# An elementwise kernel of large transfers: the second load is issued after a VectorE memset

## The chip, the cores and the metric

The kernel runs on one core of a Trainium2 chip. The metric is device time in microseconds (us) of one execution; three runs of the kernel before gave a median of 150.7 us (150.7 to 150.88). The time stands beside a profile of one further execution, taken by the hardware profiler.

## The reference

```python
B, S, D = 512, 32, 640          # bf16 x and fx, alpha one bf16 number
def reference(x, fx, alpha):
    return x + alpha * fx
```

Each input has 10,485,760 elements in bf16, so 20.97 MB of x and as much of fx are read, and 20.97 MB of output are written.

## The kernel before

The arrays are taken as flat. A **unit** is 512 bf16 numbers (1 KiB) on each of 128 partitions, 128 KiB in all; an input is 160 units. All data goes through one SBUF tile `room` of 207 units (line 83). The whole order of work is written out by hand in the string `PLAN` (lines 30 to 54), and a loop (line 114) turns each step into one instruction; no scheduler moves them. The instructions of one engine run in the order of the plan, and between engines the framework adds the waits that the data needs.

- `f 8 63 @ 152` loads units 8 to 62 of fx to places 152 and up of the room, `x ...` loads x, and `s ...` stores from the room. All of them are DMAs issued by SyncE (line 109), so they go into one queue, in this order. A word `after + 184` at the end makes the issue wait for the step `+ 184` (helper `late`, line 91).
- `a` loads alpha (line 98), sets a row `ones` with a VectorE memset of 128 numbers (line 101) and spreads alpha over the partitions with one small matmul (line 103) and a copy to `a_f` (line 104).
- `m 144 63` multiplies 63 units at place 144 by alpha, in place, on VectorE (line 122).
- `+ 0 144 38` adds 38 units at place 144 to those at place 0, on VectorE (line 144).
- `p` and `q` (lines 127 and 139) move 14 units of scaled fx aside to PSUM and add them from there.

The work is done in three stretches of the arrays, cut at units 0, 63, 124 and 160 (`CUTS`): fx is loaded and scaled, x is loaded and fx added to it, and the sum is stored from the place of x. The room is too small for all, so places are used again: the loads from the fourth large one on wait for adds that free their place. Each DMA has 128 rows, one a partition. The first steps of the plan are what matters here: a load of 8 units of fx (1 MiB) to places 144 to 151, then a load of 55 units of fx (7040 KB), alpha, 63 units of x, and 61 units of fx, none of which waits for anything.

Places 124 to 129 of the room are first written by the step `f 124 160 @ 110`, and nothing reads them before that.

Of the kernel before, what the change touches and what calls it, by code (L numbers as in the profile page):

```python
# [1 line left out]

# [4 lines left out]

ALU = mybir.AluOpType
F32 = mybir.dt.float32
I32 = mybir.dt.int32  # L10

K = 512
P = 128
ROOM = 207
CUTS = (0, 63, 124, 160)
KEPT = 14

PLAN = """  # L30
f 0 8 @ 144
f 8 63 @ 152
a
x 0 63 @ 0
m 144 63
f 63 124 @ 63
+ 0 144 38
x 63 99 @ 146
+ 38 182 25
x 99 124 @ 182  # L40
m 63 61
p 110 14
f 124 160 @ 110
+ 146 63 36
x 124 160 @ 63
+ 182 99 2
m 110 36
+ 184 101 9
s 0 63 @ 0 after + 184
q 193 14  # L50
s 63 124 @ 146
+ 63 110 36
s 124 160 @ 63
"""


@with_exitstack
def kernel(
    ctx: ExitStack,
    tc: tile.TileContext,  # L60
    x: bass.AP,
    fx: bass.AP,
    alpha: bass.AP,
    out: bass.AP,
):
    nc = tc.nc
    flat = {
        name: t.rearrange("b s d -> (b s d)") for name, t in (("x", x), ("f", fx), ("s", out))
    }
    assert flat["x"].shape[0] == P * CUTS[-1] * K  # L70

    def stretch(what, a, b):
        low, high = next(c for c in zip(CUTS, CUTS[1:]) if c[0] <= a < c[1])
        rows = flat[what][P * low * K : P * high * K].rearrange("(p n) -> p n", p=P)
        return units(rows, a - low, b - low)

    consts = ctx.enter_context(tc.tile_pool(name="consts", bufs=1))
    psum = ctx.enter_context(tc.tile_pool(name="psum", bufs=1, space=bass.MemoryType.PSUM))
    rooms = ctx.enter_context(tc.tile_pool(name="rooms", bufs=1))
    ctx.enter_context(tc.manual_schedule())  # L80

    kept = psum.tile([P, KEPT * K], x.dtype, name="kept")
    room = rooms.tile([P, ROOM * K], x.dtype, name="room")
    a_f = consts.tile([P, 1], F32, name="a_f")
    info = mybir.DependencyInfo(mybir.DependencyClass.Sync, mybir.DependencyReason.DATA)
    done, moved = [], {}

    def units(t, a, b):
        return t[:, a * K : b * K]

    def late(r, after):
        if after:
            what, a = after[1], int(after[2])
            tc.add_manual_dep(r.ins, moved[what, a].ins.name, info, reason="issued late")

    def spread_alpha(after):
        a_1 = consts.tile([1, 1], alpha.dtype, name="a_1")
        done.append(nc.sync.dma_start(out=a_1[:], in_=alpha[None, :]))  # L98
        late(done[-1], after)
        ones = consts.tile([1, P], alpha.dtype, name="ones")  # L100
        nc.vector.memset(ones[:], 1.0)  # L101
        a_ps = psum.tile([P, 1], F32, name="a_ps")
        done.append(nc.tensor.matmul(a_ps[:], ones[:], a_1[:], start=True, stop=True))  # L103
        nc.vector.tensor_copy(out=a_f[:], in_=a_ps[:])  # L104

    def transfer(what, a, b, at, after):
        away, here = stretch(what, a, b), units(room, at, at + b - a)
        out, in_ = (away, here) if what == "s" else (here, away)
        r = nc.sync.dma_start(out=out, in_=in_)  # L109
        late(r, after)  # L110
        moved[what, a] = r
        done.append(r)

    for step in PLAN.strip().split("\n"):
        what, *rest = step.split()
        if what == "a":
            spread_alpha(rest)
        elif what == "m":
            t, n = map(int, rest)
            f = units(room, t, t + n)  # L120
            done.append(
                nc.vector.tensor_scalar(out=f, in0=f, scalar1=a_f[:], scalar2=None, op0=ALU.mult)  # L122
            )
        elif what == "p":
            t, n = map(int, rest)
            done.append(
                nc.vector.tensor_scalar(  # L127
                    out=units(kept, 0, n).bitcast(I32),
                    in0=units(room, t, t + n).bitcast(I32),
                    scalar1=0,  # L130
                    scalar2=None,
                    op0=ALU.bitwise_or,
                )
            )
        elif what == "q":
            t, n = map(int, rest)
            xt = units(room, t, t + n)
            done.append(
                nc.vector.tensor_tensor(out=xt, in0=xt, in1=units(kept, 0, n), op=ALU.add)  # L139
            )  # L140
        elif what == "+":
            t, u, n = map(int, rest)
            xt, f = units(room, t, t + n), units(room, u, u + n)
            moved[what, t] = nc.vector.tensor_tensor(out=xt, in0=xt, in1=f, op=ALU.add)  # L144
            done.append(moved[what, t])
        else:
            a, b, _, at = rest[:4]
            transfer(what, int(a), int(b), int(at), rest[4:])

    last = nc.sync.nop(nofuse=True)  # L150
    for i in done[:-1]:
        tc.add_manual_dep(last.ins, i.ins.name, info, reason="all but the last store")


# [1 line left out]
_INS = ['x', 'fx', 'alpha']  # L156
_OUTS = [((512, 32, 640), 'bfloat16')]


# [23 lines left out]
```

## Time and profile before

| | us |
|---|---|
| median of three runs | 150.70 |
| the profiled execution | 150.75 |
| its span (first to last instruction of the engines) | 149.0 |
| DMA packets, as a share of 16 engines' span | 98.0% |
| bytes moved | 62.92 MB in 1586 packets |
| VectorE busy | 69.4 (47%) |

The profile page divides the span in 40 slices and gives, for each, how busy an engine is in tenths; the DMA row is the mean over the 16 DMA engines of the core. The windows view gives the same for any stretch: after the stretch and its length come the busy time of each engine with its number of instructions, then the granted TensorE clock, the DMA share and the GB/s. A packet is counted in the stretch in which it starts, with its whole size and its whole time; so a short stretch can show a share over 1, and the bytes of a stretch divided by 8192 count the packets of the first load, whose rows have 8192 bytes. In the timeline and in the chain of work, times are us from the start of the span; SPq is SyncE's sequencer, which issues the DMAs.

### The profile page before, as it was taken

To read this page: it belongs to the slowest core of one execution; us is meant where nothing else is said; L and a number is where in the kernel's file an instruction comes from. 1 tells how busy PE (TensorE), PEld (TensorE's weight loads), DVE (VectorE), ACT (ScalarE), POOL (GpSimd) and SP (SyncE) were. 2 spreads that over 40 slices of the span, in tenths; PEclk is the share of its full clock that TensorE was granted. 3 is DMA by queue.
4 is the path that set the end of the run, shared out by engine and by line. 5 is a ranking of instruction groups with operands and counts; after the bars stand their busy time and mean duration, and the time that the engine had idled before them with its cause. 6 is when DMAs were issued, how large, how long until landed. Compare 5 with 4: busy or idle time off the path is not lost.

```text
span 149.0 us, 80 instructions
## 1 busy us (share of the span) xinstructions
PE 0.2 (0%) x1; PEld 0.1 (0%) x1; DVE 69.4 (47%) x13; POOL 0.2 (0%) x4
## 2 busy tenths in 40 slices
PE   0000000000000000000000000000000000000000
PEld 0000000000000000000000000000000000000000
DVE  0000009920099996999999009999950000000000
POOL 0000000000000000000000000000000000000000
DMA  5996998996969969989999989999696998969993
GB/s 176 590 439 287 484 519 364 468 537 294 546 268 537 520 285 427 475 376 422 419 454 475 445 346 475 475 436 554 277 554 277 546 419 386 537 268 427 475 475 158
DMA packets 1586, 62.92 MB, mean 422 GB/s; under 512 B 178, under 2 KB 178, under 8 KB 178
## 3 DMA queue, kind: packets, MB, share of 16 engines
q1 hardware_dynamic: 1586, 62.92, 98.0%
HBM read 41.94 MB, written 20.97 MB: 422 GB/s over the span
## 4 chain that ended last, share of the span: by engine, by line
DMA 38%; DVE 27%; DVEq 7%; another core or an unknown queue 1%; SPq 1%; issue 0%
DMA room<-in_x_dram 26%; DVE room L144 13%; DMA room<-in_fx_dram 11%; DVE room L122 9%; DVEq L178 7%; DVE kept L127 3%; DVE room L139 2%; SPq L109 1%; SPq L98 0%; DVEq L122 0%; DVEq L144 0%
## 5 line engine op out<-in xcount | busy, mean ns | idle before, releaser
L144 DVE TENSOR_TENSOR room<-room 128x18432 bf16<-128x18432 bf16 (+4 forms) x6 | 39.7, 6641 | 10.4 <-DMA room<-in_x_dram 10.4
L122 DVE TENSOR_SCALAR room<-room,a_f 128x32256 bf16<-128x32256 bf16 (+2 forms) x3 | 22.0, 7331 | 8.4 <-DMA room<-in_fx_dram 8.3
L104 DVE COPY a_f<-a_ps 128x1 f32<-128x1 f32 x1 | 0.2, 157 | 21.1 <-PE a_ps L103 21.1
L127 DVE TENSOR_SCALAR kept<-room 128x3584 int32<-128x3584 int32 x1 | 3.9, 3894 | 0.0
L139 DVE TENSOR_TENSOR room<-room,kept 128x7168 bf16<-128x7168 bf16 x1 | 3.9, 3881 | 0.0
L101 DVE MEMSET ones<- 1x128 bf16 x1 | 0.2, 165 | 0.8 <-PEq L167 0.8
L103 PE MATMUL a_ps<-a,ones 1*128 1x1 bf16 x1 | 0.2, 158 | 21.9 <-DMA a<-in_alpha_dram 21.9
L167 POOL MEMSET const-uint8-127<- 128x1 uint8 x1 | 0.1, 102 | 0.0
L167 POOL MEMSET const-bfloat16-1.0<- 128x1 bf16 x1 | 0.1, 101 | 0.0
L103 PEld LDWEIGHTS <-ones 1*128 1x128 bf16 x1 | 0.1, 98 | 1.0 <-DVE ones L101 1.0
L167 POOL MEMSET const-float32-0.0<- 128x1 f32 x1 | 0.1, 98 | 0.2 <-issue 0.2
L167 POOL MEMSET const-float32-1.0<- 128x1 f32 x1 | 0.1, 98 | 0.0
## 6 DMA issues: line engine op xcount, KB each, us to landing
room<-in_x_dram SPq DMA_DIRECT2D x2, 4608.0 KB, 18.7
room<-in_x_dram SPq DMA_DIRECT2D x1, 8064.0 KB, 39.1
out_dram<-room SPq DMA_DIRECT2D x1, 8064.0 KB, 22.3
room<-in_fx_dram SPq DMA_DIRECT2D x1, 7808.0 KB, 57.2
out_dram<-room SPq DMA_DIRECT2D x1, 7808.0 KB
room<-in_fx_dram SPq DMA_DIRECT2D x1, 7040.0 KB, 20.9
room<-in_fx_dram SPq DMA_DIRECT2D x1, 4608.0 KB, 17.1
out_dram<-room SPq DMA_DIRECT2D x1, 4608.0 KB, 38.1
```

The costliest lines, as they stand in the source:

```text
L101: nc.vector.memset(ones[:], 1.0)
L103: done.append(nc.tensor.matmul(a_ps[:], ones[:], a_1[:], start=True, stop=True))
L104: nc.vector.tensor_copy(out=a_f[:], in_=a_ps[:])
L109: r = nc.sync.dma_start(out=out, in_=in_)
L122: nc.vector.tensor_scalar(out=f, in0=f, scalar1=a_f[:], scalar2=None, op0=ALU.mult)
L127: nc.vector.tensor_scalar(out=units(kept, 0, n).bitcast(I32), in0=units(room, t, t + n).bitcast(I32), scalar1=0, scalar2=None, op0=ALU.bit ...
L139: nc.vector.tensor_tensor(out=xt, in0=xt, in1=units(kept, 0, n), op=ALU.add)
L144: moved[what, t] = nc.vector.tensor_tensor(out=xt, in0=xt, in1=f, op=ALU.add)
L167: nc = _bacc.Bacc("TRN2", target_bir_lowering=False, num_devices=1)
L178: with _tile.TileContext(nc) as tc:
```

## The change

A new kind of step, `w t n`, clears n units from place t with a VectorE memset. One such step is put behind the first load, and the second load waits for it. Everything else in the plan stays.

```diff
 PLAN = """
 f 0 8 @ 144
-f 8 63 @ 152
+w 124 6
+f 8 63 @ 152 after w 124
 a
 x 0 63 @ 0
 m 144 63
...
                 nc.vector.tensor_scalar(out=f, in0=f, scalar1=a_f[:], scalar2=None, op0=ALU.mult)
             )
+        elif what == "w":
+            t, n = map(int, rest)
+            moved[what, t] = nc.vector.memset(units(room, t, t + n), 0.0)
         elif what == "p":
```

In the compiled program the memset is VectorE's first instruction, ahead of the memset of `ones`, and is written as 128x1536 (6 KiB a partition, so elements of 4 bytes). On SyncE the order of DMAs is the same as before, and only the second DMA has a new wait.

## The prediction

> **What bounds the kernel now.** I read the page's DMA rows first. The 16 DMA engines are busy nearly all the time, on one queue, so a gain or loss must come from the stretch before their first packet, the one behind their last, or a pause or slowness between.
>
> ```profile
> DMA  5996998996969969989999989999696998969993
> ...
> q1 hardware_dynamic: 1586, 62.92, 98.0%
> ```
>
> The reader is to see the 5 of the first slice and the 98.0%: 98.0% of 149.0 us is 146.0 us of packets on each engine, and 3.0 us without. VectorE, the only other engine with work, is busy 47%. Next the start, since the change is there: the chain of work, in order of time (start, length, what), gives SyncE's first two issues, and the timeline (the same columns) what is issued behind them.
>
> ```profile
> 0.73 0.38 SPq L109
> ...
> 1.17 0.42 SPq L109
> ```
>
> ```profile
> 0.81 0.17 DVE L101 MEMSET ones<- 1x128 bf16 x1 [0.81 <-PEq L167]
> ...
> 1.64 0.33 SPq L98 DMA_DIRECT2D a<-in_alpha_dram  x1
> 2.01 0.35 SPq L109 DMA_DIRECT2D room<-in_x_dram  x1
> 2.40 0.45 SPq L109 DMA_DIRECT2D room<-in_fx_dram  x1
> 21.87 0.16 PE L103 MATMUL a_ps<-a,ones 1*128 1x1 bf16 x1 [21.87 <-DMA a<-in_alpha_dram]
> ```
>
> Then the windows view over the first 5 us, to see when the first load's packets run and when the second's begin.
>
> ```profile
> 0.00:1.74 1.74, 0.00 (x0) 0.10 (x1) 0.17 (x1) 0.20 (x4) 1.00 0.00 0
> 1.74:2.00 0.26, 0.00 (x0) 0.00 (x0) 0.00 (x0) 0.00 (x0) 1.00 2.22 410
> 2.00:2.50 0.50, 0.00 (x0) 0.00 (x0) 0.00 (x0) 0.00 (x0) 1.00 0.65 197
> 2.50:3.00 0.50, 0.00 (x0) 0.00 (x0) 0.00 (x0) 0.00 (x0) 1.00 0.77 295
> 3.00:3.50 0.50, 0.00 (x0) 0.00 (x0) 0.00 (x0) 0.00 (x0) 1.00 1.00 410
> 3.50:4.00 0.50, 0.00 (x0) 0.00 (x0) 0.00 (x0) 0.00 (x0) 1.00 1.01 426
> 4.00:4.57 0.57, 0.00 (x0) 0.00 (x0) 0.00 (x0) 0.00 (x0) 1.00 0.98 417
> 4.57:5.10 0.53, 0.00 (x0) 0.00 (x0) 0.00 (x0) 0.00 (x0) 1.00 4.12 1778
> ```
>
> No packet starts before 1.74 us, which is 1.01 us behind the start of the first issue (0.73). GB/s times length gives the bytes started, and those over 8192 the packets of the first load: 13, 12, 18, 25, 26 and 29 in the six stretches from 1.74 on, 123 of its 128 by 4.57. The last stretch's 942 KB are the other 5 (41 KB) and 16 of 56,320 bytes (901 KB): all 16 engines go over to the second load between 4.57 and 5.10 us. That load was issued at 1.17, so its packets stood ready about 2.18 (1.17 + 1.01) and waited 2.4 us or more for the engines. **This 2.4 us is the cover of the change.**
>
> **The memset.** No row has this operation at this size. From below: the memset of `ones` took 0.165 us, and 6 KiB can't take less. From above: if all of those 165 ns went with its 128 elements, one is 1.29 ns, and 1536 are 1.98 us (3.96 us for 3072, if it went by bf16). The nearest row by element size is the int32 operation of line 127, 3894 ns for 3584, which is 1.087 ns each: 1536 x 1.087 = 1.67 us. I take 1.67. The Trainium skill ("VectorE: DVE Perf Modes", section "Zero memsets can be issued as uint32 (trn2)") says that a memset takes one cycle an element whatever the type; by its clock of 0.96 GHz an estimate is 1.60 us, and the sum would be the same.
>
> **The issue.** VectorE's first instruction starts at 0.81, so the memset ends at about 2.48. SyncE sees it a little later (the chain shows 0.02 us between the end of VectorE's line 127 at 71.93 and the issue at 71.95; I take 0.05): the second load is issued at 2.53 instead of 1.17, 1.36 us late. Its packets stand ready at 2.53 + 1.01 = 3.54. The engines take them from 4.57 on: 1.03 us are left, and the wait costs **nothing**. Without that cover it would cost up to 1.36 us.
>
> **What is queued behind the waiting instruction.** On SyncE: alpha (1.64 to about 3.00), 63 units of x (2.01 to 3.37) and 61 of fx (2.40 to 3.76). None is wanted soon. Alpha's packet comes behind the second load's on its engine and lands at 21.87, by then the issue is long past. x starts behind 8064 KB of fx: at 431 GB/s (below) 19.2 us, so at some 21 us; fx behind it near 40. On VectorE: the memset of `ones` moves from 0.81 to about 2.5, and the weight load on TensorE behind it from 1.03 to about 2.7; both wait for alpha at 21.87 anyway. VectorE's next instruction is the copy at 22.06, after 21.1 us of idleness. The cleared places are next written by a load issued at 71.95; it already waits for later VectorE steps. So the cost is nothing there too, with 17 us or more of cover.
>
> **What a later issue does to the first load's packets.** Here the trace shows something that the change could take away. DMA share times length times 16, over the packets, is the mean time of one: 0.71, 0.43, 0.34, 0.32 us in the first four stretches against 0.31 in the last two. The excess, 13 x 0.40 + 12 x 0.12 + 18 x 0.03 + 25 x 0.01 = 7.4 us, is 0.46 us on each of 16 engines. It falls in 1.74 to 3.1 us, just while SyncE issues the next four DMAs (1.17 to 2.85). Two readings: the engines start cold, or issuing disturbs them. For the second, look at issues in mid-run:
>
> ```profile
> 51.50:53.50 2.00, 0.00 (x0) 0.00 (x0) 2.00 (x2) 0.00 (x0) 1.00 1.16 500
> ...
> 71.90:73.90 2.00, 0.00 (x0) 0.00 (x0) 2.00 (x2) 0.00 (x0) 1.00 0.98 422
> 81.60:83.60 2.00, 0.00 (x0) 0.00 (x0) 0.57 (x1) 0.00 (x0) 1.00 0.77 332
> ```
>
> GB/s over share is the rate while busy: 431, 431 and 431, in stretches that begin with an issue (51.57, 71.95, 81.60), as in one without (98.60 to 101.00: 430 at 1.00). In the four stretches at the start it is 185, 303, 383 and 410. So an issue in mid-run slows nothing, though large packets may hide there what small ones show. And the issues don't go away: they move to 2.53 to 4.2 us, over the rest of the same load. I take the excess as a cold start that stays, **0**, and keep both ends: a gain of 0.46 if the whole excess is due to the issues and vanishes, a loss of as much if it comes a second time.
>
> **The sum.** 150.75 + 0 (wait, covered) + 0 (queued behind it) + 0 (packets at the start) = 150.75 in the profiled execution; against the median of 150.70, 0.05 lower, it is 150.7.
>
> **Rivals.**
> *Quiet start, faster.* With only one load issued, its 16 engines are fed sooner and more evenly. For: the coincidence in time above, and that the end is set by the engine that lags most, so an uneven start is paid in full. Against: the 431 GB/s in mid-run. It must remove 0.30 of the 0.46 us to be seen; about 0.4 gives 150.3. Chance 0.28.
> *The queue runs dry, slower.* At 4.57 to 5.10 us an engine finds no packet of the second load. This decides once memset and issue take over 1.03 us more than I reckoned: a memset over 2.70 us, or a second load that needs over 2.04 us from issue to packet. At 3.96 us for the memset the packets stand ready at 0.81 + 3.96 + 0.05 + 1.01 = 5.83, and the mean engine (dry at 4.83) waits 1.0 us: 151.7. A smaller form: the queue is not dry, but the second load's first packets are as slow as the first load's (13 x 0.40 / 16 = 0.33 us): 151.0. For: nothing here shows a queue filled with 1 us to spare. Against: 1.01 us in the only case seen, and the program's 1536 elements. Chance 0.19, mostly at 151.0 to 151.3.
> *Every delay is paid, slower.* A transfer issued 1.36 us late ends 1.36 us late, as it would where nothing covers it: 152.1. The waiting 2.4 us of the second load speak against it. Chance 0.03. The Trainium skill ("DMA: Bandwidth & Descriptors", section "Rules for kernel authors") speaks for early issue, so that the fixed setup overlaps with other work; by it the change can only lose, and the trace agrees only where a queue has nothing else to move.
> *The wait has no effect*, because the memset is over before SyncE comes to it. It would have to end by 1.17, so take 0.36 us; the time is that of the forecast, 150.7, and its chance is in there.
>
> **How the numbers follow.** A measurement of this kernel can tell about 0.2%, 0.3 us, from no change. The forecast, within 0.2%, has 0.50; faster 0.28; slower 0.19 + 0.03 = 0.22. The range goes from 150.25 (the excess at the start nearly all gone) to 151.2 (the excess twice, 150.7 + 0.46); left out are a pause of half a microsecond or more and the whole delay, about 0.1, and a gain above all that the start holds, under 0.1.
>
> **What would show it.** In the profile after: a VectorE memset from 0.8 to 2.5 us, the second issue at 2.5, and in the windows view all 16 engines going over near 4.6 to 5.1 us, with DMA shares near 1 around it. If the forecast is wrong by the quiet start, packets at 1.74 to 2.5 us show over 300 GB/s while busy; if by the dry queue, the shares from 4.6 to 6 us fall below 1. Later, every landing should keep its time (alpha 21.87, x 41.15) or shift with the start by one amount.

## The result, and the profile after

The changed kernel takes 151.49 us in the median of 22 runs (150.94 to 152.44); the kernel before, on the same chips, 150.74 (150.66 to 151.38). The ratio is 1.005, with a 95% interval of 1.0035 to 1.0064: 0.75 us slower, where I had forecast no change. The spread of the runs has grown too, from 0.7 to 1.5 us. The profiled execution took 151.35 us, its span 149.6, both 0.60 above those of before.

The DMA rows of the page look as before:

```profile
DMA  5998996997969979989999899999696997969993
...
q1 hardware_dynamic: 1586, 62.92, 98.0%
```

98.0% of a longer span is more busy time: 0.980 x 149.6 = 146.6 us a DMA engine against 146.0, for the same bytes. So the loss is not idleness in the main: the same packets took longer (0.46 us an engine of the 0.60, by the trace's packet records, which hold the start, time and size of every packet). The timeline of the first 25 us (start, length, what) shows where the steps moved:

```profile
0.72 2.09 SPq L112 DMA_DIRECT2D room<-in_fx_dram  x2
1.11 1.34 DVE L129 MEMSET room<- 128x1536 uint32 x1 [1.11 <-PEq L173]
2.41 0.17 DVE L104 MEMSET ones<- 1x128 bf16 x1
...
2.86 0.32 SPq L101 DMA_DIRECT2D a<-in_alpha_dram  x1
3.22 0.34 SPq L112 DMA_DIRECT2D room<-in_x_dram  x1
3.61 0.43 SPq L112 DMA_DIRECT2D room<-in_fx_dram  x1
22.20 0.16 PE L106 MATMUL a_ps<-a,ones 1*128 1x1 bf16 x1 [22.20 <-DMA a<-in_alpha_dram]
```

The memset ends at 2.45 us; in the trace the second issue, merged here with the first into one row of x2, starts at 2.48. All this is where I put it (2.48 and 2.53). But alpha, which comes behind the second load's packets, starts the matmul at 22.20 instead of 21.87. So 0.33 us are lost inside the first two loads. The windows view has it:

```profile
1.74:2.00 0.26, 0.00 (x0) 0.00 (x0) 0.26 (x1) 0.00 (x0) 1.00 2.78 473
2.00:2.50 0.50, 0.00 (x0) 0.00 (x0) 0.50 (x2) 0.00 (x0) 1.00 0.15 49
2.50:3.00 0.50, 0.00 (x0) 0.10 (x1) 0.08 (x1) 0.00 (x0) 1.00 1.05 410
...
4.57:5.10 0.53, 0.00 (x0) 0.00 (x0) 0.00 (x0) 0.00 (x0) 1.00 4.32 1747
```

The last row is to be read beside the same stretch of before (4.12, 1778). GB/s over share, the rate while busy, is 404 where it was 432. All 16 engines still go over to the second load between 4.57 and 5.10, without a pause, so by the record nothing is late. But the second load's first packets are **slow**. A packet of 56,320 bytes took 2.08 us in every case of before; here, by the packet records, 9 of the first 16 took longer by over 0.01 us, the slowest by 0.55, and all 16 by 0.15 on average.

The later steps, from the timelines: VectorE's first large add starts at 41.57 (before 41.25, 0.32 later), the multiplication behind the last load of fx at 89.69 (89.15, 0.54 later), and the end is 0.60 later. So just over half of the loss in this execution is there when x has landed. The rest shows after the issue at 72.29 us (before 71.95, 0.34 later). It goes with packets that run at 422 to 428 GB/s while busy in the stretches 52 to 60, 60 to 66 and 66 to 72 us, against 430 to 432 before.

### The profile page after: what moved, and what is told of

It reads as the page before. It is cut to its first block, busy times and chain, and to the rows that moved or that the text cites. A ratio compares the mean times of both kernels' runs of the same rounds, so it can differ in the third digit from the quotient of the medians.

```text
span 149.6 us, 81 instructions
## 1 busy us (share of the span) xinstructions
PE 0.2 (0%) x1; PEld 0.1 (0%) x1; DVE 70.7 (47%) x14; POOL 0.2 (0%) x4
## 4 chain that ended last, share of the span: by engine, by line
DMA 37%; DVE 28%; DVEq 7%; another core or an unknown queue 1%; issue 1%; SPq 0%
DMA room<-in_x_dram 26%; DVE room L150 13%; DMA room<-in_fx_dram 12%; DVE room L125 9%; DVEq L184 7%; DVE kept L133 3%; DVE room L145 2%; DVE room L129 1%; SPq L101 0%; SPq L112 0%; DVE ones L104 0%; DVEq L125 0%; DVEq L150 0%
## 5 line engine op out<-in xcount | busy, mean ns | idle before, releaser
L129 DVE MEMSET room<- 128x1536 uint32 x1 | 1.3, 1338 | 1.1 <-PEq L173 1.1
```

Source lines behind the costliest of these rows:

```text
L129: moved[what, t] = nc.vector.memset(units(room, t, t + n), 0.0)
```

## The experiments

**Lead** is below the time from the start of a load's issue to the start of its first packet. For the second load it was 3.41 us before (1.17 to 4.58) and is 2.19 in the changed kernel (2.48 to 4.67). My forecast stood on 1.01 us being enough. Two theories at first: *in step* (the late issue leaves the 16 engines close together, and so they slow each other) and *late* (the load is issued too near to its turn). The diffs are against the changed kernel.

### Is it the memset, the other issues, the length, or the first load?

The first kernel keeps the memset and drops the wait.

```diff
-f 8 63 @ 152 after w 124
+f 8 63 @ 152
```

> The memset of 6 KiB stays, but nothing waits for it: the second load is issued at 1.17 us as before. Theory 'in step' (with the second issue late, the 16 engines start their packets close together, and engines in step slow each other for the next 65 us): as before, 150.7 us, hardly any packet of the second load above 2.08 us. Theory 'late' (the second load is issued too near to its turn, and its first packets are slow for that): 150.7 us as well. Theory 'memset' (VectorE's writing at the start disturbs the loads): 151.5 us.

Measured: 150.87 us, ratio 0.9998 (0.999 to 1.0007). The memset is free, also where it writes while loads land.

The second one moves the wait to alpha and the two loads behind it.

```diff
-f 8 63 @ 152 after w 124
-a
+f 8 63 @ 152
+a after w 124
```

> The second load is issued at once, and alpha with the two large loads behind it wait for the memset (issues at 2.5 us and later, as in the changed kernel). Theory 'in step': the issue that falls on the first packets (1.74 to 2.5 us) is the second load's own, which is back, so the engines are spread again: 150.7 to 150.9 us. Theory 'late': the second load is early again: 150.7 us. A third theory, that issues at 2.5 to 4 us disturb the packets of that time and of the second load: 151.3 us or more, since three of the four stay late.

Measured: 150.90 us, ratio 1.0001 (0.9992 to 1.0009). The wait costs only where it stands before the second load, though the three behind it are issued at 2.49, 2.84 and 3.23 us.

The third has a memset of 2 KiB.

```diff
-w 124 6
+w 124 2
```

> The memset is 2 KiB a partition (512 elements, some 0.55 us), so the second issue comes at about 1.5 us instead of 1.17 or 2.46. Theory 'late': its packets stand ready 2 us before their turn, so 150.7 us. Theory 'in step': the second load's issue work falls on the first load's second packets instead of the first: between the two, 150.8 to 151.3 us, with a wide spread of runs.

Measured: 150.87 us, ratio 0.9998 (0.999 to 1.0007), with a lead of 3.46 us (the first load took longer in that execution). 'In step' had expected a spread of runs; there is none (150.78 to 151.07).

The fourth keeps the wait and makes the first load twice as large.

```diff
-f 0 8 @ 144
+f 0 16 @ 144
 w 124 6
-f 8 63 @ 152 after w 124
+f 16 63 @ 160 after w 124
```

> The first load is 16 units instead of 8 (its packets then last until about 7.5 us), and the second, of 47 units, still waits for the 6 KiB memset and is issued at 2.46 us. Theory 'late': the cover is 3.5 us instead of 1.1, so the loss goes: 150.7 us. Theory 'in step': the start of the first load is as undisturbed as in the changed kernel, so the engines stay close and the loss stays: 151.2 us or more, a spread of runs of over 0.8 us.

Measured: 150.89 us, ratio 0.9997 (0.9989 to 1.0006). The issue is as late as in the changed kernel, and the packets of the second load start just as close together: 15 of 16 between 7.28 and 7.52 us. But its lead is 4.65 us, and nothing is lost. **'In step' falls here, 'late' stands.**

### Is it really the lead?

With the large first load, a longer memset brings the lead back to what it was.

```diff
-f 0 8 @ 144
-w 124 6
-f 8 63 @ 152 after w 124
+f 0 16 @ 144
+w 124 15
+f 16 63 @ 160 after w 124
```

> The first load is 16 units as in the run that lost nothing, but the memset is 15 KiB a partition (to about 4.85 us), so the second issue comes 2.25 us before the turn of its packets (7.1 us), as in the changed kernel. Theory 'late': the loss comes back, 151.3 to 151.6 us, with slow first packets of the second load. If it stays at 150.9, the lead isn't what decides, but something bound to the first 5 us of the execution or to the 8 small packets per engine.

Measured: 152.05 us, ratio 1.0071 (1.0058 to 1.0084). The lead was 2.37 us, and the loss is back, larger than the 151.3 to 151.6 us expected. The windows view at the change of loads, first for the 16 units with a lead of 4.65 us, then for this kernel:

```profile
7.12:7.52 0.40, 0.00 (x0) 0.00 (x0) 0.00 (x0) 0.00 (x0) 1.00 4.47 1925
```

```profile
7.25:7.76 0.51, 0.00 (x0) 0.00 (x0) 0.00 (x0) 0.00 (x0) 1.00 4.35 1510
```

1925 / 4.47 = 431 GB/s while busy, and 1510 / 4.35 = 347. By the packet records some engines also stood idle here between the two loads, 1.6 us over all 16 together; in the changed kernel none did.

The next one doubles the memset of the changed kernel, so that the engines really run dry.

```diff
-w 124 6
+w 124 12
```

> The memset is twice as long (12 KiB a partition, to about 4.05 us); the second load is issued at 4.06 and by the first load's 1.01 us its packets stand ready at 5.07, where the engines run dry at 4.67 to 5.00. Theory 'late' (the second load must be issued some time, over 2.2 us, before its turn, or its first packets are slow): a larger loss than the changed kernel's 0.75 us, 151.9 to 152.5. Theory 'only a pause counts' (what my forecast stood on): 0.1 to 0.4 us of pause, 151.2 us, below the changed kernel. Theory 'other issues' (the descriptors of alpha and the two large loads, issued 0.4 to 1.6 us behind the second load, disturb its first packets): they fall behind the first packets' start, about 151.5.

Measured: 152.28 us, ratio 1.0091 (1.0078 to 1.0104). The issue started at 4.08, the first packet at 5.05, a lead of 0.97 us. This is the forecast's 1.01 us to the first packet, and it isn't the price. By the packet records the pause between the two loads is 0.40 us on the average engine, as I would have reckoned, but the loss is 1.4. The windows view and the timeline of this kernel:

```profile
5.05:5.90 0.85, 0.00 (x0) 0.00 (x0) 0.00 (x0) 0.00 (x0) 1.00 3.28 1060
```

```profile
42.80 17.02 DVE L150 TENSOR_TENSOR room<-room 128x19456 bf16<-128x19456 bf16 x2 [10.39 <-DMA room<-in_x_dram]
...
90.69 5.02 DVE L125 TENSOR_SCALAR room<-room,a_f 128x18432 bf16<-128x18432 bf16 x1 [6.97 <-DMA room<-in_fx_dram]
```

The row holds the 16 first packets: 0.85 x 3.28 = 2.79 us each on average, 0.71 above 2.08, at 323 GB/s while busy. The slowest, in the packet records, took 1.34 us more. x lands 1.55 us later than before (42.80 against 41.25), the last fx 1.54 (90.69 against 89.15), and the span is 1.6 longer. By the packet records, the last of the 16 first packets ended 0.43 us later than before in the changed kernel and 1.64 later in this one, and x landed 0.32 and 1.55 later. So the end goes by the slowest of 16 engines, not by their mean, and what it loses at the start it hardly makes up.

Two kernels ask whether the issues *behind* the second load do the harm. One moves them away from the start of its first packets, the other brings them up to these (the last issue ends 0.3 us before the first of them) and leaves the second load early.

```diff
 f 8 63 @ 152 after w 124
-a
+w 130 14
+a after w 130
```

> The second load waits for the 6 KiB memset as in the changed kernel (issue at 2.46), and alpha with the loads behind it wait for a second memset of 14 KiB a partition (to about 6.3 us), so that nothing else is issued while the first 16 packets of the second load start. Theory 'late': the loss stays, 151.3 to 151.6 us. Theory 'other issues': it goes, 150.9 us.

```diff
-w 124 6
-f 8 63 @ 152 after w 124
-a
+w 124 9
+f 8 63 @ 152
+a after w 124
```

> The second load is issued at once, and alpha with the two large loads wait for a 9 KiB memset (to about 3.25 us): they are issued at 3.3, 3.6 and 4.0 to 4.5 us, later than in the changed kernel, so that their descriptors come with the first packets of the second load. Theory 'late': 150.9 us. Theory 'other issues': 151.4 us or more.

Measured: 152.16 us (151.01 to 152.63), ratio 1.0078 (1.0051 to 1.0105), for the first, with a lead of 2.27; 150.88, ratio 1.0001 (0.9993 to 1.001), for the second. The first lost more than the 151.3 to 151.6 us expected of 'late', but it lost with the other issues out of the way. 'Other issues' is out.

### How long must the lead be?

```diff
-w 124 6
+w 124 4
```

> The memset is 4 KiB a partition (to about 1.92 us): the second load is issued at 1.93 us, some 2.75 us before its turn at 4.7. So far a lead of 3.3 us or more lost nothing, 2.2 us lost 0.6 to 1.3 us, 1.0 us lost 1.4 us. Theory 'late': between, 150.9 to 151.4 us, with few slow first packets. Theory 'only a pause counts': 150.9 us.

Measured: 151.88 us, ratio 1.0068 (1.0056 to 1.008), at a lead of 2.77 us. The expectation of a loss between missed its size: it is not below that of the changed kernel.

```profile
4.71:6.15 1.44, 0.00 (x0) 0.00 (x0) 0.00 (x0) 0.00 (x0) 1.00 1.64 643
```

The stretch again holds just the 16 first packets: 643 / 1.64 = 392 GB/s while busy. By the packet records one engine started on the second load only at 6.10 us, 0.86 behind the last of the others, and stood idle before. The last of the 16 packets ended 1.27 us later than before, and the timeline has x landing 1.20 later (42.45).

```diff
-w 124 6
+w 124 3
```

> The memset at the start is 3 KiB a partition (768 elements, to about 1.65 us): the second load is issued at about 1.66, some 3.05 us before its turn at 4.7. If the loss sets in as a step between 2.75 us (which lost 1.0 us) and 3.3 us (nothing): either 150.9 or 151.7 us. If it is the tail of slow engines that grows as the lead shrinks: 150.9 to 151.2 us, with one to four slow packets of 16.

Measured: 150.90 us, ratio 1.0002 (0.9992 to 1.0013), at a lead of 3.07 us.

```profile
4.75:5.15 0.40, 0.00 (x0) 0.00 (x0) 0.00 (x0) 0.00 (x0) 1.00 5.41 2314
```

2314 / 5.41 = 428 GB/s. So nearly all of the loss sets in between 3.07 and 2.77 us. Whether as a step is not decided: by the packet records two of the 16 first packets took longer than 2.08 us, by up to 0.17, as the expectation of a growing tail had it too. And a lead is that of one execution: in eight traces with the second issue at 1.16 or 1.17 us it came out between 3.41 and 3.67. Two of the 12 runs, the profiled one among them, took 151.5; in that trace most of the excess lies at 52 to 72 us, as the second part of the changed kernel's does.

### Only at the start, and only for loads?

In mid-run, a memset over the place of a load delays its issue while VectorE has nothing else that is wanted soon. The start is that of the kernel before.

```diff
-w 124 6
-f 8 63 @ 152 after w 124
+f 8 63 @ 152
...
 + 146 63 36
+w 63 15
 x 124 160 @ 63
```

> The start is that of the kernel before. In mid-run the load of x units 124 to 160 is made late: a memset of 15 KiB a partition over its place, some 4.0 us while VectorE is idle anyway, comes before it, so it is issued at about 85.6 instead of 81.6 us, 2.4 us before its turn at 88.0. Theory 'late' as a general rule for loads (packets of a load issued less than about 3 us ahead start on time but slowly): slow first packets at 88 us and 151.5 to 152.1 us. Rival 'only at the cold start': 150.9 us.

> As the run before, but the memset in mid-run is 7 KiB a partition (some 1.9 us): issue at about 83.5, 4.5 us before the turn. Theory 'late': nothing lost, 150.9 us. If it loses as much as its neighbour, the cause is the memset or what moves on VectorE (the add behind it), not the lead.

> The memset in mid-run is 11 KiB a partition (2.93 us): the load of x units 124 to 160 is issued at about 84.7, 3.4 us before its turn at 88.15. If the lead that is needed is the same as at the start (under 3.3 us): 150.9 us. If it is longer beside large packets in mid-run (a queue must work off more before it comes to the new load): 151.2 us or more, with slow first packets at 88 us.

The other two have `w 63 7` and `w 63 11` in its place. The load is issued at 85.82, 83.73 and 84.70 us. Measured: 152.28 us, ratio 1.0103 (1.0085 to 1.0121), somewhat above the 151.5 to 152.1 expected, at a lead of 2.33 us; 150.93, ratio 1.0003 (0.9994 to 1.0011), at 4.49; 150.95, ratio 1.0005 (0.9996 to 1.0013), at 3.57. The windows view over the 16 first packets of that load, for the leads of 2.33, 4.49 and 3.57 us:

```profile
88.15:89.32 1.17, 0.00 (x0) 0.00 (x0) 0.15 (x1) 0.00 (x0) 1.00 1.59 504
```

```profile
88.21:88.77 0.56, 0.00 (x0) 0.00 (x0) 0.00 (x0) 0.00 (x0) 1.00 2.45 1053
```

```profile
88.26:88.66 0.40, 0.00 (x0) 0.00 (x0) 0.00 (x0) 0.00 (x0) 1.00 3.43 1475
```

317 GB/s while busy, then 430 and 430. It is no matter of the cold start: the second load lost time at leads up to 2.77 us and not from 3.07 on, and this one lost at 2.33 and not from 3.57 on. In mid-run no other issue can be the cause either, since nothing is issued behind this load until 96.68 us. Mostly its packets start on time and run slowly, but not all: by the packet records the engines stood idle for 1.6 us over all 16 together before it at the lead of 2.33 us, and not at the other two.

The number of packets still ahead in the queue doesn't decide. By the packet records, 2.0 an engine had not started yet when the load with 11 KiB was issued, and nothing was lost; in the changed kernel it was 7.0. The bytes not yet started would sort the kernels as well as the time does (those with up to 0.94 MB lost, those with 1.05 MB or more didn't), since the queue drains at a nearly steady rate. These two were not told apart.

The last one delays a store, which reads from SBUF.

```diff
-w 124 6
-f 8 63 @ 152 after w 124
+f 8 63 @ 152
...
-s 0 63 @ 0 after + 184
+w 99 4
+s 0 63 @ 0 after w 99
```

> The start is that of the kernel before. The first store, which reads from the chip's own memory, is issued later: a memset of 4 KiB a partition (some 1.1 us) comes before it, so its issue moves from 96.67 to about 97.75 us, and the lead before its turn at 99.0 us from 2.4 to 1.3 us. VectorE's later steps move by 1.1 us, under cover of the stores. In the kernel before the lead of 2.4 us cost its first packets nothing. If the lead is needed for the reading of HBM only: 150.9 us. If any transfer needs some 3 us: slow packets at 99 us and 151.3 us or more.

Measured: 150.90 us, ratio 1.0000 (0.9991 to 1.0009).

```profile
99.13:99.64 0.51, 0.00 (x0) 0.00 (x0) 0.51 (x1) 0.00 (x0) 1.00 4.70 2024
```

The store was issued at 97.97, a lead of 1.17 us to the first packet, and ran at 2024 / 4.70 = 431 GB/s. The lead was needed by both loads from HBM, and not by this store.

| kernel | lead, us | rate of the first 16 packets while busy, GB/s | median, us |
|---|---|---|---|
| long wait | 0.97 | 323 | 152.28 |
| changed kernel | 2.19 | 404 | 151.49 |
| changed, the rest later | 2.27 | 388 | 152.16 |
| late load in mid-run | 2.33 | 317 | 152.28 |
| 16 units, later | 2.37 | 347 | 152.05 |
| 4 KiB | 2.77 | 392 | 151.88 |
| 3 KiB | 3.07 | 428 | 150.90 |
| before | 3.41 | 432 | 150.74 to 150.88 |
| 2 KiB | 3.46 | 432 | 150.87 |
| mid-run, 11 KiB | 3.57 | 430 | 150.95 |
| mid-run, 7 KiB | 4.49 | 430 | 150.93 |
| 16 units | 4.65 | 431 | 150.89 |

No kernel beat the one before: those that lose nothing lie within 0.1 us of it.

## Why the prediction was wrong

- **What bounds the kernel**: right. All of it is DMA time, and a slow stretch of packets at the start moves every later step by about as much.
- **The memset and the second issue**: right. The ends of the rows are 2.45 and 2.48 us against 2.48 and 2.53.
- **The wait, "1.03 us are left, and the wait costs nothing"**: this step failed. I took 1.01 us, from an issue to the first packet's start, as the time until a load's packets "stand ready". The start of a packet in the record isn't that: in the changed kernel each engine takes the packet up on time and then works on it slowly. The term that was mis-sized is the lead that a load needs, which lies between 2.77 and 3.07 us, by one trace each, in place of 1.01. The cover was 3.41 us from the issue on, not 2.4 from the packets on, and the change took 1.2 of it.
- **What is queued behind it**: right. Their delay alone costs nothing (150.90 and 150.88 us).
- **The packets at the start**: I held both halves of the answer here. The first load's packets, too, start at 1.74 and run slowly until 3.1 us, 2.4 us behind their issue. I put that down as a cold start that stays, not as what another load may show too when it isn't issued well ahead. The rates of 431 GB/s in mid-run didn't speak against it, since they lay beside loads whose lead was 5 to 7 us.
- **The rivals**: the smaller form of the dry queue, "the second load's first packets are as slow as the first load's", is what happened, and no pause came with it in the changed kernel. I gave it little, and I priced it by the mean of 16 engines: 0.33 us. The mean excess was smaller still, 0.15 us on the first packets, but the slowest engine sets the time: 0.32 us when x has landed, and 1.55 us in the long wait, where the mean was 0.71. The sign that I had named, shares that fall below 1, could not have shown this, since a slow packet counts as busy. The quiet start didn't come: by the packet records the first load's packets held 0.51 us of excess an engine, against 0.47.

What bears on the lead beyond the traces: the Trainium skill ("DMA: Bandwidth & Descriptors", section "Latency and other measured facts") gives 0.2 us for an access to HBM on average and 2 us under high load. An estimate from that page's 2 us and the 1.01 us to the first packet is 3.0 us, which lies between the two leads measured. The store, whose reads don't go to HBM, needed no such lead. No run here measured an HBM access itself, so why a load needs the lead stays open.

Two more things stay open. Why a lead of 2.77 us lost more than one of 2.19 is one: all five runs with 2.77 took 151.7 us or more, and in its trace two engines end equally late, one that stood idle and one whose first packet took 3.36 us; a single trace can't say whether that is the rule. The other is the changed kernel's second part, some 0.2 to 0.3 us from packets between 52 and 72 us that run at 422 to 428 GB/s. The long wait has none of it, the 3 KiB kernel shows it in its profiled execution with hardly a loss at the start, and two of the 22 runs of the kernel before (151.36 and 151.38) are 0.6 us high, as that execution is. It may be a matter of how the engines stand to each other in time; nothing was tried on it.

## What to carry to other kernels

In this kernel a load that must follow another without loss had to be issued some 3 us before the queue came to it, at the start and in mid-run alike. The start of its first packet doesn't tell whether it was, and the share of busy DMA engines hides it. Compare the rate while busy (GB/s over share) over the first packets of each load with that of the next ones. And price a lag by the slowest of the 16 engines, since each carries its own rows to the end.

## What I had not expected of the hardware

Most of the loss sets in within 0.3 us of lead: at 3.07 us the first packets run at 428 GB/s and nothing is lost in the median, at 2.77 us they run at 392, with 1.0 us lost; at 0.97 us it is 1.4 us.

The start of a memset's row is not when VectorE became free. With nothing else ahead of it, the row begins at 0.91, 1.01, 1.11 and 1.43 us for 512, 1024, 1536 and 3072 elements, and ends at 1.39, 1.92, 2.45 and 4.05. The ends grow by 1.04 ns an element, the row's length by 0.84 only. The cost is to be taken from the ends.
